# Top-k attention and two feed-forward layers: the second layer of token chunk 1 in float16 parts, and the weight splits reordered

## The chip, the cores and the metric

The kernel runs on one core of one Trainium2 chip. The metric is device time in microseconds, as a median over runs. A core has a matrix engine (TensorE, PE in the rows; its weight loads are shown apart as PEld), VectorE (DVE), ScalarE (ACT), GpSimd (POOL), and a queue (SP) from which all transfers are issued here. Each engine works through its own instructions in order and waits on the others by semaphores.

## The reference

Attention over 4 batches, 8 heads, 576 positions and head size 64 keeps the 32 largest scores of each row. Its output, 2304 tokens of width 512, goes through a gated layer of width 1536 and then a squared-ReLU layer of width 2048.

```
scores = scale * q @ k.T                       # (4, 8, 576, 576)
kth = the 32nd largest of each row
attn = softmax(scores where scores >= kth)
x = (attn @ v) as (2304, 512)
x = (sigmoid(x @ w_gate) * (x @ w_val)) @ w_out      # 512 -> 1536 -> 512
r = max(x @ w_in, 0);  out = (r * r) @ w_out2        # 512 -> 2048 -> 512
```

Everything is float32 at the interface.

## The kernel before

Tokens are worked in twelve chunks (`CHUNKS`): chunks 0 to 5 of 128 tokens, chunks 6 to 11 of 256. For each chunk the attention gives x transposed, 128 x 4 x N, and then two feed-forward layers follow: here called layer 1 (weights `wg`, `wv`, `wo`) and layer 2 (`wi`, `w2`, the latter for `w_out2`).

There are two forms of these layers. `moe32` (L982) works chunks 0 and 1 (`PLAIN`) with float32 products straight from the float32 weights. `moe` (L862) works the others: each float32 operand is there as two float16 parts, high and low, scaled by powers of two, and each product is three float16 products (`SPLIT`: high by high, high by low, low by high). In layer 2 of both forms eight pairs of blocks of 128 hidden units are passed (`l2_pair`, L931 in `moe` and L1048 in `moe32`), and their squared ReLU is multiplied with `w2` (`l2_acc`). `moe` keeps three pairs in hand before it sums (`DEPTH2`), `moe32` one. Lines 938 and 959 are the two products of layer 2 in `moe`; lines 1052 and 1069 are those in `moe32`, and line 1045 is the copy between layer 1 and layer 2 there. In `moe`, lines 911 and 912 write the two parts of layer 2's input x2. For chunks from 6 on x2 is scaled by a bound that `x_norm` (L800) gets from the squares of x (`x_squares`, L789); for chunks 2 to 5 a fixed power of two (`X2B`) is used.

The weights come first as float32 pairs of blocks (`conv`, names `wg_c`, `wi_c` and so on; 34 pairs: 6 of wg, 6 of wv, 6 of wo, 8 of wi, 8 of w2). `scale` finds a power of two for each matrix. `split` (L714) makes the float16 parts of one pair, names `wg_w`, `wi_w` and so on (w2's pairs appear as `w_c` and `w_w`): ACT writes the high part (L718), and then DVE the low part (L721) or, for every third split (`LOP`), POOL in two steps (L723, L724). A pair and its parts are buffers of the same size in one pool of 35 (`WSLOTS`); the parts need a free one, and the pair's buffer comes free when it has been split and read by everyone. The first two pairs of wo lie in another pool of three buffers, tag `m4`, where x of the chunks lies as well (`x_plain` for chunks 0 and 1, then `xt_2`, `xt_3` and so on).

The order of all work is found when the program is built: instructions are emitted with priorities, and a scheduler with a simulated time line places them in each engine's order. The loop at the end of the program (from L1338) interleaves three streams by hand-set times: steps of the weights (`weight_step`), units of the attention (`att`, one block of 128 rows and one head) and steps of `moe32` (`body`). The counter `n` counts the steps of a chunk's body: 6 pairs of layer 1, 8 pairs of layer 2, one end. The list `todo` says at which step of chunk 1 each split is emitted; the splits have a time far behind (`SUP`), so they fill in where engines are free. Before, wg and wv come from step 2, wo from step 3, wi from step 8 and w2 from step 9 on. What is left is emitted after chunk 1. Chunks 2 to 11 follow in the last loop, with the attention kept ahead of them.

In the attention each row block needs four MAX8 and three MATCH_REPLACE8 on DVE (L434, L435) for its 32 largest scores, transposes on TensorE that pass through a PSUM pool of two buffers (`ps_t`, tag `tr`), and the product with v, which passes through the same pool and is then copied into x by ACT (`values`, copy at L594).

Of the kernel before, what the change touches and what calls it, by code (L numbers as in the profile page):

```python
# [72 lines left out]
PB = 10  # L73
XF = 2
# [17 lines left out]
def tile_topk_attention__then__two_moe_layers(  # L92
# [694 lines left out]
    x2s = {}  # L787

    def x_squares(ci, xt, after=None):  # L789
# [3 lines left out]
        ins = nc.scalar.activation(sq, xt[:, 0], AF.Square)  # L793
# [6 lines left out]
    def x_norm(ci, sq, N, after=None):  # L800
# [61 lines left out]
    def moe(ci, nxt=None):  # L862

        m = ahead.pop(ci)
        tts, N, ix, l1_pair = chunks[ci], m.N, m.ix, m.l1_pair
        accs = []

        def l1_acc(fp, gh):
            if not accs:
                for h in range(2):  # L870
                    accs.append(ps_a.tile([P, 512], F32, tag="acc", name=f"acc1_{ci}_{h}"))

            last = fp == NF1 // 2 - 1
            for e, d in sorted(
                ((e, d) for e in range(2) for d in range(KM)),
                key=lambda t: (t[1], t[0]) if last else t,
            ):
                f = 2 * fp + e
                if True:
                    for x, (a, b_) in enumerate(SPLIT):  # L880
                        nc.tensor.matmul(  # L881
                            accs[d // 2][:, (d % 2) * N : (d % 2 + 1) * N],
                            wblk("wo", a, f, d * P, P),
                            gh[:, b_, e * N : (e + 1) * N],
                            start=(f == 0 and x == 0 and d % 2 == 0),
                            stop=(f == NF1 - 1 and x == 2),
                            skip_group_check=True,
                        )

        queue = m.queue  # L890
        depth = max(1, len(queue))
        for fp in range(len(queue), NF1 // 2):
            queue.append((fp, l1_pair(fp)))
            yield
            if len(queue) > depth:
                l1_acc(*queue.pop(0))
        while len(queue) > 1:
            l1_acc(*queue.pop(0))
        if nxt:
            nxt()  # L900
        l1_acc(*queue.pop(0))

        pool, kw = (wpool, {"tag": "w"}) if ci >= X2W else (mpool, {"tag": "m4", "bufs": M4})
        x2 = pool.tile([P, 2, KM, N], F16, name=f"x2_{ci}", **kw)
        KH = KM // 2
        srcs = [a[:, 0 : KH * N].rearrange("p (d n) -> p d n", d=KH) for a in accs]
        with tc.high_priority(offset=XUP):
            sy, iy = x2s.pop(ci, (float(2.0**-X2B), float(2.0**X2B)))
            for h in range(2):
                hs = slice(h * KH, (h + 1) * KH)  # L910
                nc.scalar.activation(x2[:, 0, hs], srcs[h], AF.Copy, scale=sy)
                nc.vector.scalar_tensor_tensor(
                    x2[:, 1, hs], srcs[h], sy, x2[:, 0, hs], op0=ALU.mult, op1=ALU.subtract
                )
        if nxt:
            for _ in range(NPRE - 1):
                nxt()
# [61 lines left out]
        yield  # L979


    def moe32(ci, xt):  # L982
# [60 lines left out]
        l1_acc(*prev)  # L1043
        x2 = xt
# [60 lines left out]
    def attention():  # L1105
# [62 lines left out]
        def tail(n, after=None):  # L1168
# [277 lines left out]
```

## Time and profile before

| | us |
|---|---|
| median of 3 runs | 1189.3 (1188.53 to 1190.75) |
| the profiled execution, time | 1192.72 |
| the profiled execution, span from first to last instruction | 1190.9 |
| busy in the span: TensorE | 1150.0 (97%) |
| DVE | 912.2 (77%) |
| ACT | 796.2 (67%) |
| POOL | 831.5 (70%) |
| mean granted clock of TensorE | 0.991 |

Busy times count each engine's instructions; matmuls are pipelined, so the length of one matmul is longer than the distance from its start to the next one's start. A float32 product shows as two records. The rows further down come from the page, from the tables by stretch, from the time lines of single engines and from the groups by line or tile. In a time line a row with x16 stands for sixteen instructions in a run; its second number is from the first start to the last end.

### The profile page before, as it was taken

The page shows a single profiled execution, that of the slowest core. Times are in us where ns is not written, and L with a number is a line of the kernel's source. Part 1 is how long each engine was busy: PE and PEld are TensorE (multiplying, and loading weights), DVE is VectorE, ACT ScalarE, POOL GpSimd, SP SyncE. Part 2 cuts the span into 40 slices and gives each one's busy share as a digit, 9 for nine tenths or more (in the row PEclk, how much of TensorE's full clock was granted, in tenths as well). Part 3 has the DMA queues.
Part 4 walks back from the last instruction along what each step waited for, and adds up shares of the span by engine and source line. Part 5 has one row for each costly group of instructions (what it writes and reads, how often), then busy time and mean ns, then how long its engine had stood idle before and what let it go on. Part 6 is the DMA issues. An engine that isn't in the chain of part 4 may idle for free.

```text
span 1190.9 us, 30480 instructions
## 1 busy us (share of the span) xinstructions
PE 1150.0 (97%) x11457; PEld 936.0 (79%) x11457; DVE 912.2 (77%) x1905; ACT 796.2 (67%) x1681; POOL 831.5 (70%) x1294
## 2 busy tenths in 40 slices
PE   7879999999999999999999999999999999999998
PEld 5668878978878878787887688868876886886785
DVE  5998789899998998999998899999799966110000
ACT  5999985778787787767677776777577665222122
POOL 1888874688877797969778887886698668224233
PEclk9888999999999999999999999999999999999999
DMA  7997854225435667765576576555255323000000
GB/s 228 364 362 251 311 159 128 80 71 154 122 104 132 134 155 159 173 140 137 120 161 132 132 189 123 138 126 125 61 119 116 78 57 61 19 1 1 19 1 18
DMA packets 241395, 153.64 MB, mean 129 GB/s; under 512 B 191329, under 2 KB 207713, under 8 KB 241249
## 3 DMA queue, kind: packets, MB, share of 16 engines
q1 hardware_dynamic: 241248, 151.70, 49.2%
q8 instruction: 90, 1.47, 0.5%
q14 instruction: 57, 0.46, 0.1%
HBM read 105.25 MB, written 18.09 MB: 104 GB/s over the span
## 4 chain that ended last, share of the span: by engine, by line
PE 52%; SPq 1%; POOL 1%; DMA 1%; issue 1%; ACT 1%; DVE 0%; POOLq 0%; ACTq 0%
PE ph L938 11%; PE acc L959 11%; PE acc L881 7%; PE pg L841 7%; PE pv L841 7%; PE sp L423 3%; PE xp L559 3%; PE qpt L383 1%; SPq L344 1%; DMA kst<-ks 1%; PE kpt L197 0%; DVE W L435 0%; SPq L214 0%; DVE mx L434 0%; PE xn L803 0%
## 5 line engine op out<-in xcount | busy, mean ns | idle before, releaser
L434 DVE MAX8 mx<-W 128x8 f32<-128x576 f32 x432 | 327.5, 758 | 10.4
L435 DVE MATCH_REPLACE8 W<-mx,W 128x576 f32<-128x576 f32 x288 | 213.7, 742 | 0.0
L938 PE MATMUL ph<-x,wi_w 128*128 128x256 f16 (+1 forms) x1920 | 190.7, 251 | 0.0
L959 PE MATMUL acc<-w_w,rh 128*128 128x512 f16 x768 | 181.1, 379 | 1.4 <-POOL rh L951 1.4
L938 PEld LDWEIGHTS <-wi_w 128*128 128x128 f16 x1920 | 154.9, 98 | 24.6 <-issue 0.7
L506 POOL TENSOR_TENSOR pp<-S,pp 128x512 f16<-128x512 f32 x192 | 137.1, 736 | 1.9
L423 PE MATMUL sp<-kst,qt 128*128 128x288 f32 x608 | 130.1, 327 | 4.5 <-ACT S L426 3.1
L460 ACT ACTIVATE S<-S,mx 128x576 f32<-128x576 f32 x144 | 111.8, 776 | 33.5 <-DVE mx L434 32.5
L959 PEld LDWEIGHTS <-rh 128*128 128x128 f16 x768 | 72.3, 98 | 74.9 <-POOL rh L951 2.2
L841 PEld LDWEIGHTS <-wg_w 128*128 128x128 f16 x1440 | 118.1, 98 | 15.8 <-issue 1.1
L881 PEld LDWEIGHTS <-wo_w 128*128 128x128 f16 x1440 | 118.0, 98 | 14.8 <-issue 1.8
L841 PEld LDWEIGHTS <-wv_w 128*128 128x128 f16 x1440 | 117.1, 98 | 15.0 <-issue 2.6
L853 DVE TENSOR_TENSOR th<-pv,th 128x512 f32<-128x512 f32 (+1 forms) x60 | 34.6, 576 | 118.5 <-PE pv L841 110.5
L434 DVE MAX8 mx<-S 128x8 f32<-128x576 f32 x144 | 107.1, 744 | 21.2 <-ACT S L426 21.0
L426 ACT COPY S<-sp 128x576 f32<-128x576 f32 x144 | 91.8, 638 | 45.2 <-PE sp L423 22.1
L504 POOL TENSOR_SCALAR S<-S,bs 128x576 f32<-128x576 f32 x96 | 71.9, 749 | 52.1 <-ACT pp L503 45.8
L435 DVE MATCH_REPLACE8 W<-mx,S 128x576 f32<-128x576 f32 x144 | 106.9, 742 | 0.0
L950 POOL TENSOR_TENSOR r<-r 128x512 f32<-128x512 f32 (+1 forms) x80 | 70.5, 881 | 49.1 <-ACT rh L949 47.4
L841 PE MATMUL pv<-xs,wv_w 128*128 128x256 f16 x864 | 104.7, 273 | 0.0
L503 ACT ACTIVATE pp<-S,bs 128x576 f16<-128x576 f32 x96 | 74.5, 776 | 44.4 <-DVE bs L499 22.1
L841 PE MATMUL pg<-xs,wg_w 128*128 128x256 f16 x864 | 104.0, 273 | 0.0
L881 PE MATMUL acc<-gh,wo_w 128*128 128x256 f16 (+1 forms) x1056 | 102.5, 248 | 0.0
(240 smaller groups left out, 2307.0 us busy)
## 6 DMA issues: line engine op xcount, KB each, us to landing
kst<-ks SPq DMA_DIRECT2D x112, 288.0 KB, 3.2
v<-vd SPq DMA_DIRECT2D x32, 320.0 KB, 3.4
wi_r<-in_moe_w_in_dram SPq DMA_DIRECT2D x16, 512.0 KB, 5.0
w_r<-in_moe_w_out_dram SPq DMA_DIRECT2D x16, 512.0 KB, 4.9
qn<-in_q_dram SPq DMA_DIRECT2D x124, 64.0 KB, 2.6
v<-in_v_dram SPq DMA_DIRECT2D x28, 256.0 KB, 2.8
wg_r<-in_moe_w_gate_dram SPq DMA_DIRECT2D x12, 512.0 KB, 5.9
wv_r<-in_moe_w_val_dram SPq DMA_DIRECT2D x12, 512.0 KB, 7.8
```

The source lines that it names most:

```text
L423: nc.tensor.matmul(sp[:, e, 0:HALF], l, r, start=(x == 0), stop=(x == len(ops) - 1))
L426: nc.scalar.copy(ss.rearrange("p (e s) -> p e s", e=2), sp[:, :, 0:HALF])
L434: return nc.vector.max(m8, st.cur).ins
L435: ins = nc.vector.match_replace(st.wk, m8, st.cur, NEG).ins
L460: nc.scalar.activation(wk, wk, AF.Prelu, bias=kth, scale=-1.0, alpha=1.0 / BIG)
L503: nc.scalar.activation(pp[:, 0:S], wk, AF.Copy, scale=rz)
L504: nc.gpsimd.tensor_scalar(wk, wk, rz, 1.0, op0=ALU.mult, op1=ALU.mult)
L506: nc.gpsimd.tensor_tensor(pp[:, o : o + e - f], wk[:, f:e], pp[:, f:e], op=ALU.subtract)
L841: nc.tensor.matmul(pp[:, e * N : (e + 1) * N], wblk(wd, a, c, f0, P), xs[:, b_, c, :], start=(e == 0 and n == 0), stop=(n == 3 * KM - 1), ...
L881: nc.tensor.matmul(accs[d // 2][:, (d % 2) * N : (d % 2 + 1) * N], wblk("wo", a, f, d * P, P), gh[:, b_, e * N : (e + 1) * N], start=(f == ...
L938: nc.tensor.matmul(ph[:, e * N : (e + 1) * N], wblk("wi", a, c, f0, P), x2[:, b_, c, :], start=(e == 0 and n == 0), stop=(n == 3 * KM - 1) ...
L959: nc.tensor.matmul(acc2[i][:, 0:DM], gh[:, b_, e * N + i * P : e * N + (i + 1) * P], wblk("w2", a, f, 0, DM), start=(f == 0 and x == 0), s ...
```

## The change

Chunk 1 (`SPLIT2`) keeps its float32 layer 1. Its layer 2 now runs the code of `moe`, which is moved into a function `layer2` for that. The result of layer 1 is scaled by `f`, a product of powers of two from the norm of chunk 1's x and the scales of wv and wo, and written as two float16 parts over x's own buffer (two ACT and two DVE operations on halves, where one ACT copy was). The norm comes from `x_squares` and `x_norm`, which are now called for chunk 1 as well when its x is complete.

Chunk 1 thus needs wi and w2 split before its layer 2. The list `todo` is emitted along both chunks, with `n2` = 15 steps for chunk 0: wi from step 10 of chunk 0 (`SWI`), w2 from step 1 of chunk 1 (`SW2`), wg and wv from step 2 of chunk 1 and wo from step 3 as before. Entries with the same step keep the order in which they are listed, so wo's first pair is the nineteenth entry; before it was the fifth.

```diff
+SPLIT2 = (1,)
+SWI = 10
+SW2 = 1
...
-        ins = nc.scalar.activation(sq, xt[:, 0], AF.Square)
+        ins = nc.scalar.activation(sq, xt if ci in SPLIT2 else xt[:, 0], AF.Square)
...
-        t = xsmall[ci]
+        if ci in SPLIT2:
+            t = mpool.tile([P, 8], I32, tag="xsc", bufs=3, name=f"xn_{ci}s")
+        else:
+            t = xsmall[ci]
         cm = t.bitcast(F32)[:, 3:4]
         nc.vector.reduce_max(cm, pq[:, 0:N], axis=AX.X)
+        if ci in SPLIT2:
+            xnorm[ci] = pow2_scale(cm, t)
+            return
...
+    def layer2(ci, x2, ix, iy):
...
         l1_acc(*prev)
+        if ci in SPLIT2:
+            s, ix = xnorm.pop(ci)
+            sv, so = (scales[n][0] for n in ("wv", "wo"))
+            f = wsmall.bitcast(F32)[:, 21:22]
+            nc.vector.scalar_tensor_tensor(
+                f, s, float(2.0 ** -(TB + X2B)), sv, op0=ALU.mult, op1=ALU.mult
+            )
+            nc.vector.tensor_tensor(f, f, so, op=ALU.mult)
+            x2 = xt.rearrange("p c n -> p (c n)").bitcast(F16).rearrange(
+                "p (a c n) -> p a c n", a=2, c=KM
+            )
+            src = accs[0][:, 0 : KM * N].rearrange("p (d n) -> p d n", d=KM)
+            KH = KM // 2
+            for h in range(2):
+                hs = slice(h * KH, (h + 1) * KH)
+                nc.scalar.activation(x2[:, 0, hs], src[:, hs], AF.Copy, scale=f)
+                nc.vector.scalar_tensor_tensor(
+                    x2[:, 1, hs], src[:, hs], f, x2[:, 0, hs], op0=ALU.mult, op1=ALU.subtract
+                )
+            yield from layer2(ci, x2, ix, float(2.0**X2B))
+            return
...
                     if pr.ci in PLAIN:
                         xsp[pr.ci] = pr.xt
+                        if pr.ci in SPLIT2:
+                            x_squares(pr.ci, pr.xt)
...
+    n2 = n1 + NF2 // 2 + 1
+    for i in range(len(pairs_of["wi"])):
+        todo.append((max(SWI, n1 + 2 * (i // 2) + 2), "wi", i))
+    for i in range(len(pairs_of["w2"])):
+        todo.append((n2 + SW2 + i // 2, "w2", i))
     for i in range(len(pairs_of["wg"])):
-        todo.append((2 * (i // 2) + 2, "wg", i))
-        todo.append((2 * (i // 2) + 2, "wv", i))
+        todo.append((n2 + 2 * (i // 2) + 2, "wg", i))
+        todo.append((n2 + 2 * (i // 2) + 2, "wv", i))
     for i in range(len(pairs_of["wo"])):
-        todo.append((i + 3, "wo", i))
-    for i in range(len(pairs_of["wi"])):
-        todo.append((n1 + 2 * (i // 2) + 2, "wi", i))
-    for i in range(len(pairs_of["w2"])):
-        todo.append((n1 + i + 3, "w2", i))
-    todo = [(max(t[0], TD), *t[1:]) for t in todo]
+        todo.append((n2 + i + 3, "wo", i))
     todo.sort(key=lambda x: x[0])
...
-                if ci == PLAIN[-1]:
-                    at(tm - SUP)
-                    while todo and todo[0][0] <= n:
-                        split(*todo.pop(0)[1:])
+                at(tm - SUP)
+                while todo and todo[0][0] <= n + n2 * (ci == PLAIN[-1]):
+                    split(*todo.pop(0)[1:])
```

## Rows read from the trace of the kernel before

**Rows 1.** Engines by stretch: busy us (x count), granted clock, DMA share, GB/s.

```profile
140.00:280.00 140.00, 139.36 (x1150) 116.20 (x1150) 120.14 (x228) 104.10 (x204) 98.43 (x134) 1.00 0.42 120
280.00:540.00 260.00, 248.70 (x3464) 215.60 (x3464) 242.17 (x534) 198.84 (x474) 207.40 (x372) 1.00 0.59 142
540.00:1010.00 470.00, 469.54 (x4608) 371.39 (x4605) 419.28 (x878) 331.87 (x692) 373.45 (x614) 1.00 0.53 117
1010.00:1191.00 181.00, 177.13 (x1414) 136.27 (x1413) 11.15 (x20) 41.50 (x66) 55.49 (x55) 1.00 0.04 11
```

**Rows 2.** Timelines (start us, length us, engine, line) around the input of chunk 2.

```profile
181.58 1.09 PE L586 MATMUL xp<-PT,v 128*64 128x128 f32 x16
...
200.37 3.08 DVE L721 SCALAR_TENSOR_TENSOR wo_w<-wo_c,wsmall,wo_w 128x1024 f16<-128x1024 f32 x1 [0.27 <-ACT wo_w L718]
...
204.42 0.27 ACT L594 COPY xt<-xp 128x128 f32<-128x128 f32 x1
...
240.22 1.18 POOL L783 TENSOR_TENSOR xt<-xt 128x512 f16<-128x512 f32 x1
...
275.70 0.50 PE L841 MATMUL pg<-xt,wg_w 128*128 128x128 f16 x6
```

**Rows 3.** Groups of PE by line, 237 to 280: count, busy us, mean ns.

```profile
L1052 PE MATMUL ph<-x_plain,wi_c 128*128 128x128 f32 x128 | 16.5, 276 | 0.1
L1069 PE MATMUL acc<-w_c,rr 128*128 128x512 f32 x32 | 15.3, 594 | 0.0
```

**Rows 4.** Timeline of PE, second layer of chunk 1, three runs in a row.

```profile
247.38 1.95 PE L1052 MATMUL ph<-x_plain,wi_c 128*128 128x128 f32 x16
249.17 1.88 PE L1069 MATMUL acc<-w_c,rr 128*128 128x512 f32 x4
250.89 0.38 PE L1052 MATMUL ph<-x_plain,wi_c 128*128 128x128 f32 x2
```

**Rows 5.** Timeline of PE, second layer of chunk 2, two runs and what follows.

```profile
322.63 2.41 PE L938 MATMUL ph<-x,wi_w 128*128 128x128 f16 x40
324.85 0.77 PE L423 MATMUL sp<-kst,qt 128*128 128x288 f32 x4
...
333.30 2.75 PE L959 MATMUL acc<-w_w,rh 128*128 128x512 f16 x12
335.89 0.61 PE L938 MATMUL ph<-x,wi_w 128*128 128x128 f16 x8
```

**Rows 6.** Groups of PE by line, 320 to 355 (chunk 2).

```profile
L938 PE MATMUL ph<-x,wi_w 128*128 128x128 f16 x192 | 13.0, 219 | 0.0
L959 PE MATMUL acc<-w_w,rh 128*128 128x512 f16 x48 | 11.9, 380 | 0.0
```

**Rows 7.** Tile acc: count, ns min/median/max, first and last start us.

```profile
L911 ACT ACTIVATE x<-acc x8: 363/392/418, 320.6 to 531.5; 128x256 f16<-128x256 f32 x8
L912 DVE SCALAR_TENSOR_TENSOR x<-acc,x x8: 405/412/425, 321.8 to 532.8; 128x256 f16<-128x256 f32 x8
```

**Rows 8.** The page's groups: idle us ahead of the sums of layer 2.

```profile
L959 PE MATMUL acc<-w_w,rh 128*128 128x512 f16 x768 | 181.1, 379 | 1.4 <-POOL rh L951 1.4
```

**Rows 9.** Line 718, the splits on ACT: count, ns, first and last start us.

```profile
L718 ACT ACTIVATE wi_w<-wi_c,wsmall x8: 1148/1149/1151, 258.2 to 310.6; 128x1024 f16<-128x1024 f32 x8
L718 ACT ACTIVATE w_w<-w_c,wsmall x8: 1133/1149/1157, 265.0 to 324.6; 128x1024 f16<-128x1024 f32 x8
L718 ACT ACTIVATE wg_w<-wg_c,wsmall x6: 1148/1150/1156, 167.5 to 235.9; 128x1024 f16<-128x1024 f32 x6
L718 ACT ACTIVATE wo_w<-wo_c,wsmall x6: 1134/1149/1150, 199.2 to 253.0; 128x1024 f16<-128x1024 f32 x6
```

**Rows 10.** Timeline of ACT, the third and the fourth split.

```profile
174.37 1.15 ACT L718 ACTIVATE wg_w<-wg_c,wsmall 128x1024 f16<-128x1024 f32 x1
...
197.40 1.15 ACT L718 ACTIVATE wv_w<-wv_c,wsmall 128x1024 f16<-128x1024 f32 x1 [1.10 <-PE pg L997]
```

**Rows 11.** Weight loads of the float16 second layer, ns min/median/max.

```profile
L938 PEld LDWEIGHTS <-wi_w x1920: 95/98/105, 321.4 to 1176.4; 128*128 128x128 f16 x192
```

More of the change, by code (lines that the diff above doesn't have):

```diff
@@ L787, in tile_topk_attention__then__two_moe_layers @@
     x2s = {}
+    xnorm = {}
     def x_squares(ci, xt, after=None):
@@ L860, in moe_head @@
         m.N, m.ix, m.l1_pair = N, ix, l1_pair
[L862 to L917, printed above, removed]
@@ L918, in moe @@
+    def layer2(ci, x2, ix, iy):
+        tts = chunks[ci]
+        N = len(tts) * P
         usc, i2 = layer2_scales()
@@ L979, in moe, with l1_acc @@
         yield
+    def moe(ci, nxt=None):
+        m = ahead.pop(ci)
+        N, ix, l1_pair = m.N, m.ix, m.l1_pair
+        accs = []
+        def l1_acc(fp, gh):
+            if not accs:
+                for h in range(2):
+                    accs.append(ps_a.tile([P, 512], F32, tag="acc", name=f"acc1_{ci}_{h}"))
+            last = fp == NF1 // 2 - 1
+            for e, d in sorted(
+                ((e, d) for e in range(2) for d in range(KM)),
+                key=lambda t: (t[1], t[0]) if last else t,
+            ):
+                f = 2 * fp + e
+                if True:
+                    for x, (a, b_) in enumerate(SPLIT):
+                        nc.tensor.matmul(
+                            accs[d // 2][:, (d % 2) * N : (d % 2 + 1) * N],
+                            wblk("wo", a, f, d * P, P),
+                            gh[:, b_, e * N : (e + 1) * N],
+                            start=(f == 0 and x == 0 and d % 2 == 0),
+                            stop=(f == NF1 - 1 and x == 2),
+                            skip_group_check=True,
+                        )
+        queue = m.queue
+        depth = max(1, len(queue))
+        for fp in range(len(queue), NF1 // 2):
+            queue.append((fp, l1_pair(fp)))
+            yield
+            if len(queue) > depth:
+                l1_acc(*queue.pop(0))
+        while len(queue) > 1:
+            l1_acc(*queue.pop(0))
+        if nxt:
+            nxt()
+        l1_acc(*queue.pop(0))
+        pool, kw = (wpool, {"tag": "w"}) if ci >= X2W else (mpool, {"tag": "m4", "bufs": M4})
+        x2 = pool.tile([P, 2, KM, N], F16, name=f"x2_{ci}", **kw)
+        KH = KM // 2
+        srcs = [a[:, 0 : KH * N].rearrange("p (d n) -> p d n", d=KH) for a in accs]
+        with tc.high_priority(offset=XUP):
+            sy, iy = x2s.pop(ci, (float(2.0**-X2B), float(2.0**X2B)))
+            for h in range(2):
+                hs = slice(h * KH, (h + 1) * KH)
+                nc.scalar.activation(x2[:, 0, hs], srcs[h], AF.Copy, scale=sy)
+                nc.vector.scalar_tensor_tensor(
+                    x2[:, 1, hs], srcs[h], sy, x2[:, 0, hs], op0=ALU.mult, op1=ALU.subtract
+                )
+        if nxt:
+            for _ in range(NPRE - 1):
+                nxt()
+        yield from layer2(ci, x2, ix, iy)
     def moe32(ci, xt):
@@ L1043, in moe32 @@
         l1_acc(*prev)
+        if ci in SPLIT2:
[8 more added lines that the diff above has]
+                "p (a c n) -> p a c n", a=2, c=KM
+            )
+            src = accs[0][:, 0 : KM * N].rearrange("p (d n) -> p d n", d=KM)
+            KH = KM // 2
+            for h in range(2):
+                hs = slice(h * KH, (h + 1) * KH)
+                nc.scalar.activation(x2[:, 0, hs], src[:, hs], AF.Copy, scale=f)
+                nc.vector.scalar_tensor_tensor(
+                    x2[:, 1, hs], src[:, hs], f, x2[:, 0, hs], op0=ALU.mult, op1=ALU.subtract
+                )
+            yield from layer2(ci, x2, ix, float(2.0**X2B))
+            return
         x2 = xt
```

## The prediction, made before the change was run

> **What bounds the kernel now.** The median is 1189.3 us; the profiled execution took 1192.7 us, of which the span is 1190.9. All durations below come from that execution, so sums are made against 1192.7 and then carried to the median, 3.4 us lower. I read the busy time of the engines by stretch first. The reader is to see that TensorE (PE) is idle for 0.6 us of the 140 us between 140 and 280, for 11.3 us of the 260 between 280 and 540, for 0.5 us of the 470 after that, and that its granted clock is 1.00 in all four stretches, the higher level of 2.4 GHz [rows 1]. VectorE (DVE) has 20 us to spare in the first of these stretches and 51 us in the third, and after 1010 it does 11 us of work in 181. So from about 140 us on TensorE has a backlog, and the time after that point is the sum of its work plus some 16 us of gaps. Whatever is taken from TensorE there comes off the end, unless it turns into a gap.
>
> That the backlog is real is seen at chunk 2: the low part of its input, the last thing that its first layer needs from the attention, is written at 240.22 + 1.18 = 241.4 us, and its first product is issued at 275.70 [rows 2]. TensorE is 34 us behind its supply.
>
> **The change part by part.**
>
> *Second layer of chunk 1 in float16 parts.* This layer lies between 237 and 280 us, inside the stretch where TensorE never rests. Before, it has 64 float32 products of 128 columns and 16 of 512. Each shows as two records: 128 and 32 records in this stretch [rows 3]. Their pace, from start to start in an unbroken run: 16 records in 249.17 - 247.38 = 1.79 us, 0.112 each, and 4 in 250.89 - 249.17 = 1.72 us, 0.430 each [rows 4]. So 128 x 0.112 + 32 x 0.430 = 14.3 + 13.8 = 28.1 us. After, it has 3 products for each: 192 of 128 columns and 48 of 512. Chunk 2, which has the same 128 tokens and already runs this code, shows the pace: 40 in 324.85 - 322.63 = 2.22 us, 0.0555 each, and 12 in 335.89 - 333.30 = 2.59 us, 0.216 each [rows 5]. So 192 x 0.0555 + 48 x 0.216 = 10.7 + 10.4 = 21.0 us. Saved: 7.1 us. The groups by line say the same in another way, with the overlaps at the ends of runs counted in: 16.5 + 15.3 = 31.8 us [rows 3] against 13.0 + 11.9 = 24.9 us [rows 6], 6.9 us. I take 7.1, the pace: how often the schedule switches between kinds of products after the change is not known.
>
> *The norm of x for chunk 1.* Four products of 128 columns with ones, 4 x 0.0555 = 0.2 us. The squaring on ScalarE (ACT), one reduction and the tiny scale operations run between the arrival of x for chunk 1 and its use after the whole first layer; they are needed only at the start of the second layer, so I cost them at nothing. Without that cover they would cost one hand-over more, as priced next.
>
> *From layer 1 to layer 2.* One ACT copy becomes two ACT copies and two DVE operations on halves; chunk 2's show 0.39 us for each of the first and 0.41 for each of the second [rows 7]. TensorE needs the high half at once and the low half 8 products later. Bounds: 0, if score products and transposes fill the place as they do at chunk 2, and 2 x 0.39 + 2 x 0.41 = 1.6 us in a row, with as much again for the search operations that DVE has queued ahead: 3.2 us. I take 0.5, near the lower end, since at chunk 2 there is attention work in that very place.
>
> *Per pair of blocks.* ACT squares once more and POOL subtracts once more, eight times; TensorE has three pairs in hand before it needs a result (DEPTH2 = 3, against one before), and the ten chunks that run this code, 80 pairs, show 1.4 us of TensorE idle ahead of these sums in all [rows 8], so nothing is added.
>
> *The splits, moved.* All 34 stay, with the same work: ACT 1.15 us each [rows 9], then DVE, or POOL for every third. The order changes: wi goes first, from step 10 of chunk 0, then w2 is mixed with wg, wv and wo. No DMA moves. Before, three splits are issued by 174.37 and the next at 197.40 [rows 10]: the three free weight buffers are taken, and the next comes free only when chunk 1 has read wg and wv. After, wi can be split right behind chunk 0's last use of it and gives its buffer back, so this hole of 23 us can hold splits (some five or six: between 197.4 and 253.0 the other 15 of the 18 splits of wg, wv and wo were issued, one in 3.7 us [rows 9, 10]). The cost: ACT, DVE and POOL are fuller between 165 and 250 and emptier between 265 and 326, where w2 and most of wi were split [rows 9]. TensorE is not touched directly. But one queue is: the split of wo's first pair, now fifth, becomes nineteenth. Chunk 2's input lives in the buffer that this pair gives back: the product that fills it is begun at 181.58, the split runs from 200.37 to 203.45, and the copy into xt starts only at 204.42 [rows 2]. Behind this copy stand a PSUM buffer of two, hence all transposes of the attention. When the attention stalls there, DVE and ACT are free for splits, so the eleven that would still be due at 197 (nineteen less three and five) would go at little over ACT's 1.15 us each; I expect the copy some 10 us later. TensorE has 34 us of backlog to cover that, less 7. Without that cover each us late would cost one.
>
> Sum: -7.1 + 0.2 + 0.5 + 0 = -6.4: 1186.3 for a profiled execution, 1182.9 for the median, called 1183.0.
>
> **The rivals.**
>
> *Late input, slower.* If the wo split is not sped up by the stall, 11 splits at 3.7 us from 197 put it at 238, and with it the copy some 35 us late. Chunk 2 is reached 7 us earlier, and attention products that are held back (what the second layer leaves of TensorE between 237 and 280: 43 - 31.8 = 11 us, a quarter [rows 3]) let it come earlier still, so TensorE runs dry when the delay D passes (34 - 7)/1.26 = 21 us, and each further us costs 1.26. The point from which the kernel is slower by over 0.2% is a gap of 6.4 + 2.4 = 8.8 us, D = 28. Half way from there to the worst, D = 31.5, the gap is 13.2 us: 1183.0 + 13.2 = 1196.2. For it: the order of the list. Against: before, the splits hurried in exactly such a stall. Chance 0.11.
>
> *DVE takes over, no change.* Between 280 and 540 DVE is busy 242 of 260 us [rows 1]. If a TensorE that is 7 us early only waits there for scores and transposed weights, the gaps of 11.3 us grow by 5 or so: about 1188.0. Against: the splits leave this stretch at the same time. Chance 0.12.
>
> *Weight loads set the pace, no change.* Three float16 products need 192 weight loads where the float32 layer had 128. A float16 load lasts 98 ns [rows 11]. If products came at the pace of their loads, 192 x 0.098 = 18.8 us plus 10.4 makes 29.2 against 28.1: 1.1 us lost, 1190.6. Against it stand 40 products in 2.22 us. This is the change not doing what it says. Chance 0.04. The Trainium skill, "TensorE: Matmul & The Clock Gate", section "Back-to-back issue gap", gives about 81 ns a product for a sustained stream of weight loads and products at 128 columns, and about 131 ns at 512. By its first figure the 192 products would take 15.6 us and the gain would be 2 us; by both together 21.8 us and a gain of about 6. The trace disagrees with both figures: 55.5 and 216 ns [rows 5].
>
> *More than the products.* Chunk 2's second layer begins at 321 [rows 7] while w2 is still being split, until about 326 [rows 9]. With wi and w2 done early, ACT, DVE and POOL serve chunk 2 and the search better, and a third of the 11.3 us of gaps could go: 1179.3. Chance 0.16.
>
> **How the numbers follow.** The forecast itself, 1183.0 within 2.5 us either way (the bounds of the hand-over and of the norm), has 0.57. Faster, by over 0.2% (2.4 us, about what a measurement of this kernel can tell from no change): 0.57 + 0.16 = 0.73. Within 0.2%: 0.12 + 0.04 = 0.16. Slower: 0.11. The range of 1178.5 to 1190.5 takes in the larger gain and both cases of no change but not the late input; it leaves out about 0.15.
>
> **What would show it.** TensorE's busy time falls by about 7 us; the lines of the second layer show 128 float32 records instead of 256 and 32 instead of 64; runs of 128 columns keep 55.5 ns. TensorE's gaps between 140 and 280 stay under 2 us; chunk 2's first product comes near 269. The first copy into xt comes before 224. I am wrong if gaps in front of chunk 2's products by a split or by x appear, if the gaps between 280 and 540 grow by as much as the products saved, or if the span falls by much more than TensorE's busy time.

## The result and the profile after

The changed kernel takes 1204.69 us (median of 4 runs, 1203.02 to 1206.72) against 1190.03 for the kernel before, run beside it: a ratio of 1.0117, interval 1.0096 to 1.0137. It is slower by 14.7 us, where 1183.0 was forecast. Its profiled execution took 1206.72 us with a span of 1204.9, against 1190.9. The ratios here and below are worked out from the single executions of both kernels and need not equal the quotient of the two medians. In two kernels below one execution was far longer than all others (4846.01 and 1899.15 us), and these two are left out of the medians.

The engines by stretch of the changed kernel, answering to [rows 1] (columns: stretch, its length, busy us and count of PE, PEld, DVE, ACT and POOL, granted clock, DMA share, GB/s):

```profile
140.00:280.00 140.00, 126.20 (x1139) 106.95 (x1138) 122.50 (x213) 106.59 (x201) 116.54 (x128) 0.96 0.38 107
280.00:540.00 260.00, 248.90 (x3416) 214.41 (x3414) 236.04 (x539) 191.85 (x469) 191.00 (x374) 0.99 0.59 145
540.00:1010.00 470.00, 468.06 (x4642) 374.77 (x4641) 421.90 (x886) 331.00 (x694) 367.32 (x605) 1.00 0.53 118
```

The loss stands in the first row. TensorE was idle there for 0.6 us and is now idle for 13.8; GpSimd went from 98.4 us of work to 116.5; the granted clock fell from 1.00 to 0.96. The later rows hardly differ from before: gaps of 11.1 us against 11.3 between 280 and 540, 1.9 against 0.5 after that. In finer slices of the same view:

```profile
180.00:200.00 20.00, 17.80 (x128) 14.56 (x129) 17.69 (x35) 13.18 (x23) 14.28 (x13) 0.83 0.38 96
200.00:220.00 20.00, 16.14 (x126) 15.71 (x125) 18.73 (x25) 14.30 (x21) 19.66 (x17) 0.91 0.31 86
220.00:240.00 20.00, 18.39 (x173) 17.00 (x172) 18.12 (x30) 14.48 (x25) 17.06 (x17) 1.00 0.30 76
240.00:260.00 20.00, 16.00 (x175) 14.06 (x174) 19.83 (x39) 17.20 (x34) 14.54 (x19) 1.00 0.33 83
```

GpSimd is full in 200 to 220 (19.66 of 20). What TensorE waited for between 160 and 280 (total us, times, longest), the four largest:

```profile
PE acc L1038 <- DVE g L1028: 4.7, 2, 3.9
PE sp L426 <- POOL qt L402: 3.9, 2, 2.8
PE sp L426 <- ACT qt L398: 2.6, 2, 1.5
PE ph L895 <- ACT x_plain L1074: 1.4, 1, 1.4
```

In the first two the longest wait leads back to a split on GpSimd. Here is that of the second, in the time line of the changed kernel (start us, length us, engine, line; the bracket is the idle time before, and who ended it). L724 is the low part of a split on VectorE, L727 on GpSimd, L402 a small step of the attention (`qt`, the low part of the queries) that TensorE's scores need:

```profile
176.63 1.27 DVE L724 SCALAR_TENSOR_TENSOR wi_w<-wi_c,wsmall,wi_w 128x1024 f16<-128x1024 f32 x1
176.66 3.24 POOL L727 TENSOR_TENSOR wi_w<-wi_c,wi_w 128x1024 f16<-128x1024 f32 x1
178.50 2.49 DVE L724 SCALAR_TENSOR_TENSOR wi_w<-wi_c,wsmall,wi_w 128x1024 f16<-128x1024 f32 x1
179.86 1.59 POOL L1099 TENSOR_TENSOR rr<-r 128x256 f32<-128x256 f32 x1
181.42 0.72 POOL L402 TENSOR_TENSOR qt<-qn,qt 128x256 fp32r<-128x256 f32 x1
182.20 1.09 PE L426 MATMUL sp<-kst,qt 128*128 128x288 f32 x3 [2.81 <-POOL qt L402]
```

The split holds GpSimd from 176.66 to 179.90, a step of chunk 0's layer 2 follows, and only then comes the 0.72 us for which TensorE stands still for 2.81 us. The longest of the first is of the same kind, with VectorE between. L1026 and L1028 make the gate and the gated product `g` that the sums of layer 1 (L1038) need:

```profile
204.55 3.09 POOL L727 TENSOR_TENSOR w_w<-w_c,w_w 128x1024 f16<-128x1024 f32 x1
207.61 0.40 POOL L1026 TENSOR_SCALAR th<-th 128x256 f32<-128x256 f32 x1
208.05 0.42 DVE L1028 TENSOR_TENSOR g<-pg,th 128x256 f32<-128x256 f32 x1 [1.07 <-POOL th L1026]
208.53 3.68 PE L1038 MATMUL acc<-g,wo_c 128*128 128x128 f32 x16 [3.86 <-DVE g L1028]
```

The layer itself did what it was meant to do. Its two groups (count, busy us, mean ns, idle us before), answering to [rows 3] and [rows 6]:

```profile
L895 PE MATMUL ph<-x_plain,wi_w 128*128 128x128 f16 x192 | 13.7, 219 | 1.4 <-ACT x_plain L1074 1.4
L916 PE MATMUL acc<-w_w,rh 128*128 128x512 f16 x48 | 12.1, 380 | 0.0
```

And the input of chunk 2, answering to [rows 2]:

```profile
218.55 0.27 ACT L597 COPY xt<-xp 128x128 f32<-128x128 f32 x1 [1.42 <-DVE wo_w L724]
...
263.21 1.16 POOL L786 TENSOR_TENSOR xt<-xt 128x512 f16<-128x512 f32 x1
...
282.27 0.50 PE L851 MATMUL pg<-xt,wg_w 128*128 128x128 f16 x6
```

The first copy comes 14 us later than before, but the finished input still waits 18 us for TensorE. It is not what TensorE ran dry on; between 160 and 280 TensorE waited 0.5 us in all for a copy into xt.

### The profile page after: what moved, and what is told of

Its sections match the earlier page's. It is cut to its first block, busy times and chain, and to the rows that moved or that the text cites. A ratio compares the mean times of both kernels' runs of the same rounds, so it can differ in the third digit from the quotient of the medians.

```text
span 1204.9 us, 30687 instructions
## 1 busy us (share of the span) xinstructions
PE 1149.3 (95%) x11541; PEld 937.5 (78%) x11541; DVE 917.5 (76%) x1915; ACT 799.0 (66%) x1691; POOL 840.5 (70%) x1302
## 5 line engine op out<-in xcount | busy, mean ns | idle before, releaser
L916 PE MATMUL acc<-w_w,rh 128*128 128x512 f16 x816 | 194.5, 379 | 0.1
L895 PEld LDWEIGHTS <-wi_w 128*128 128x128 f16 x2112 | 166.6, 98 | 28.1 <-issue 2.0
L916 PEld LDWEIGHTS <-rh 128*128 128x128 f16 x816 | 76.5, 98 | 76.0 <-POOL rh L908 0.8
L907 POOL TENSOR_TENSOR r<-r 128x512 f32<-128x512 f32 (+1 forms) x88 | 75.4, 857 | 48.5 <-ACT rh L906 46.7
L426 PEld LDWEIGHTS sp<-kst,qt 128*128 128x128 f32 x608 | 89.7, 191 | 19.1 <-POOL qt L402 4.8
```

The source lines that it names most:

```text
L426: nc.tensor.matmul(sp[:, e, 0:HALF], l, r, start=(x == 0), stop=(x == len(ops) - 1))
L895: nc.tensor.matmul(ph[:, e * N : (e + 1) * N], wblk("wi", a, c, f0, P), x2[:, b_, c, :], start=(e == 0 and n == 0), stop=(n == 3 * KM - 1) ...
L907: nc.gpsimd.tensor_tensor(r, r, r, op=ALU.mult)
L916: nc.tensor.matmul(acc2[i][:, 0:DM], gh[:, b_, e * N + i * P : e * N + (i + 1) * P], wblk("w2", a, f, 0, DM), start=(f == 0 and x == 0), s ...
```

## The experiments

Two questions were put: which part of the change costs, and where the 7 us of products went. All times below are medians beside runs of the kernel before on the same chip (1189.7 to 1191.0), each followed by the ratio and its 95% interval.

### Each part alone

The float16 layer alone, with the splits in the order of before (`todo` as before; layer 2 of chunk 1 reads parts that exist by then):

```diff
+    def otherblk(name, a, kt, f0, n):
+        return wblk("wg", a, kt % KM, f0 % 512, n)
...
+        blk = otherblk if ci in SPLIT2 else wblk
```

> Chunk 1's second layer runs the float16 code of the changed kernel, but the splits keep the order and the steps of the kernel before; since wi and w2 are not yet split then, this layer reads parts of wg in their place (its output rows are left wrong). Theory (the splits stand in front of small operations in the queues of POOL, DVE and ACT while they are packed into 165 to 265 us): the layer by itself saves what was worked out, about 6 us, so 1182 to 1187, and TensorE is idle for under 3 us between 160 and 280. Rival 1 (the layer itself, its norm, its hand-over and its extra ACT and POOL work, brings the gaps): 1195 or more, with gaps between 160 and 280. Rival 2 (chunk 2's input comes late because of wo's first pair): here the pair is split as before, so 1182 to 1187 too.

Measured: 1189.62, ratio 0.9997 (0.9978 to 1.0015). The layer by itself brings nothing that can be measured; the 3 to 8 us expected did not come, and neither did the loss of the first rival.

The splits alone, with chunk 1's float32 layer 2 on constants (the same is done for `w2`):

```diff
-SPLIT2 = (1,)
+SPLIT2 = ()
...
-                        fblk("wi", c, (2 * fp + e) * P, P),
+                        ident if ci == PLAIN[-1] else fblk("wi", c, (2 * fp + e) * P, P),
```

> The splits stand where the changed kernel has them, but chunk 1's second layer stays in float32 products of the same count and shape; since wi and w2 are already split and their float32 pairs gone, it reads constants in their place (its output rows are left wrong). Theory: gaps and slow clock between 160 and 250 as in the changed kernel and no products saved, so about 1204.7 + 6.5 = 1211, range 1206 to 1214. Rival 1 (the layer brings the gaps): about 1189 to 1192. Rival 2 (late input): 1208 to 1214 as well, it differs in the run with wo's first pair in front.

Measured: 1202.85, ratio 1.0095 (1.0075 to 1.0114), below the range of 1206 to 1214 but far above the rival's. Nearly the whole loss belongs to the moved splits. TensorE's longest wait in this trace is another one than in the changed kernel: 6.4 us for a step of VectorE (`kn`, the low part of the keys), which stands in VectorE's own queue behind a split that lasts 2.42 us beside one on GpSimd:

```profile
201.89 3.17 POOL L727 TENSOR_TENSOR w_w<-w_c,w_w 128x1024 f16<-128x1024 f32 x1
203.71 2.42 DVE L724 SCALAR_TENSOR_TENSOR wv_w<-wv_c,wsmall,wv_w 128x1024 f16<-128x1024 f32 x1
206.73 0.67 DVE L211 TENSOR_TENSOR kn<-kpt,kp 128x512 fp32r<-128x512 f32 x1
207.45 0.36 PE L200 MATMUL kpt<-ident,ke 64*128 64x64 f32 x1 [6.44 <-DVE kn L211]
```

So it is not one small step, nor GpSimd's queue alone, that the packed splits hold up.

### What in the splits costs

None of the splits on GpSimd (`LOA = 34` in place of 0, changed kernel):

> The changed kernel, but no split uses POOL: all low parts are written by DVE (LOA = 34). Theory, in the form that POOL splits of 3.3 us and more stand ahead of POOL's small steps (the query parts, the gate) and that DVE and POOL stretch each other's splits when they overlap: the gaps that end on POOL go, TensorE's idle time between 160 and 280 falls from 13.8 to about 6 us, 1193 to 1198. Rival (DVE is simply overfull there, whoever splits): DVE gets 10 more low parts of 1.27 us, the gaps stay or grow: 1204 to 1215.

Measured: 1191.59, ratio 1.0009 (0.9990 to 1.0027): 13 us of the 14.7 come back, more than expected. But this edit also plans the order anew, and it brings the first copy into xt back to 206.5 us.

wo's first pair split early again, as in the kernel before:

```diff
-        todo.append((n2 + i + 3, "wo", i))
+        todo.append((n2 + i + 3 if i else 9, "wo", i))
```

> The changed kernel, with wo's first pair split first instead of nineteenth, so that chunk 2's first x is not held back for it. Rival 2 (the late copy into xt and the transposes behind it hold the attention up, and this costs TensorE): 1190 to 1198, the copy into xt near 204. Theory (the queues): the gaps ahead of 218 stay; 1202 to 1207.

Measured: 1194.36, ratio 1.0029 (1.0010 to 1.0047), with the first copy into xt back at 203.9 us. The edit gave back 10 us, which is the range of the late copy and not that of the queues. Yet it shifts which splits are every third one, and the order of everything behind; so this run alone proves nothing on wo, and it does not refute the late copy either.

GpSimd's splits in four pieces each, so that small steps might pass between them (changed kernel):

```diff
-            nc.gpsimd.tensor_scalar(c, c, s, 1.0, op0=ALU.mult, op1=ALU.mult)
-            nc.gpsimd.tensor_tensor(t[:, 1], c, t[:, 0], op=ALU.subtract)
+            for e in range(2):
+                for q in range(2):
+                    cs = c[:, e, q * 256 : (q + 1) * 256]
+                    hi, lo = (t[:, a, e, q * 256 : (q + 1) * 256] for a in range(2))
+                    nc.gpsimd.tensor_scalar(cs, cs, s, 1.0, op0=ALU.mult, op1=ALU.mult)
+                    nc.gpsimd.tensor_tensor(lo, cs, hi, op=ALU.subtract)
```

> The changed kernel, but each split on POOL is cut into four pieces of 128x256, so that POOL's small steps need to wait for 0.3 to 0.6 us of a split instead of 2.1 to 3.2. The work on POOL and what DVE and POOL take from each other when both split stays the same. Theory that the stall is a matter of queue order (a small step of POOL stands behind a whole split): most of what the run without POOL splits gained comes here too, 1192 to 1197. Rival (DVE and POOL slow each other down, and the sum of the work is too much): 1201 to 1206.

Measured: 1207.26, ratio 1.0144 (1.0111 to 1.0177), above both ranges. Shorter single steps did not help here, though this order too is planned anew. The wait for `qt` grows from 3.9 us to 7.5:

```profile
PE sp L426 <- POOL qt L402: 7.5, 3, 4.3
```

and GpSimd is full for longer (the last busy figure of each stretch):

```profile
180.00:200.00 20.00, 17.30 (x125) 13.61 (x124) 16.35 (x31) 13.10 (x23) 19.22 (x28) 0.93 0.38 103
200.00:220.00 20.00, 18.38 (x138) 18.11 (x139) 16.72 (x26) 13.73 (x22) 19.39 (x31) 0.83 0.28 74
```

No splits on GpSimd, and the hand-over from layer 1 to layer 2 at high priority (the loop over its halves inside `with tc.high_priority(offset=int(AUP * 50))`):

> The changed kernel without POOL splits, and with the four steps that write chunk 1's x2 emitted at high priority, so that no split and no search step stands ahead of them. In the run without POOL splits TensorE waited 1.65 us for the second high half and 1.30 us for a low half, with a slower clock behind it. Theory (each gap in this stretch costs its length): 3 to 4 us less than that run, 1187 to 1189. Rival (gaps here are made up or come back later): 1191 to 1193.

Measured: 1191.85, ratio 1.0021 (1.0002 to 1.0040). The hand-over still cost 1.7 and 1.3 us of waits; nothing was gained, and as the waits did not shrink, what a quicker hand-over is worth stays open.

The control, the same `LOA = 34` in the kernel before:

> The kernel before with all 34 splits' low parts on VectorE (none on GpSimd), the control for the same edit on the changed kernel, which took that one from 1204.7 to 1191.6. If GpSimd's share hurts only where splits are packed into the first chunk (my reading), before has nothing to win: 1188 to 1193. If a split on GpSimd costs anywhere, before becomes faster too: 1180 to 1186, and the 13 us are then not all the change's. If VectorE is short in 190 to 330, it becomes slower: 1194 or more.

Measured: 1188.13, ratio 0.9985 (0.9966 to 1.0004). Splits on GpSimd cost little or nothing where they stood before; as far as two kernels with orders of their own can tell, most of the 13 us of the third run are the change's own.

Every edit so far changes the planned order of all engines, which is a cause of its own (below). So the next kernels were changed after the order was set: every engine keeps its instructions in the same sequence, and only the sizes of some are cut. First the changed kernel, GpSimd's splits shortened (the scaling to 64 of 1024 columns, the subtraction to 512 words that leave zeros):

```diff
+    for blk in nc.m.functions[0].blocks:
+        for n, x in enumerate(blk.instructions):
...
+            if x.opcode == "TensorTensor" and _re.match(r"(wi|w2|wg|wv|wo)_w\d", m):
...
+                blk.instructions[n] = _dc.replace(x, ins=[h, h], outs=[o])
```

> The changed kernel with every engine's instructions in the changed kernel's order; only the sizes of GpSimd's split instructions are changed after the order is set: the scaling to 64 of 1024 columns, and the subtraction to one over 512 words that leaves zeros (so these weights have no low part). That takes some 2.2 us off each of 11 splits on GpSimd. If GpSimd's time in splits is what costs (small steps of attention behind them, and VectorE slowed beside them): 1190 to 1196, the gaps of 160 to 280 fall from 13.8 to under 6 us, VectorE's splits back near 1.3 us. If the order that is planned around 16 more splits in the first two chunks is what costs, whatever they take: 1200 to 1206. Between the two, both have a share, and the number gives it.

Measured: 1190.04, ratio 0.9991 (0.9970 to 1.0012): the whole loss is gone, with not one instruction in another place. So the price was GpSimd's time in the splits, as the new order places them, and what follows from it; beside the 1189.62 of the same layer in the old order, the new order by itself shows no cost. Two things were not run: the same shortening in the kernel before, so how much of the 15 us would come off there too is known only from the control above; and a kernel with the first copy into xt held late but the splits short (here it comes at 207.6), so against the late copy there are only the waits read above. No wait for `qt` on GpSimd is left between 160 and 280; the longest that remains is again for `g`:

```profile
PE acc L1038 <- DVE g L1028: 2.5, 1, 2.5
```

This run's stretches 180 to 240 and 240 to 300:

```profile
180.00:240.00 60.00, 56.10 (x490) 51.22 (x489) 56.75 (x103) 49.14 (x85) 35.91 (x50) 0.97 0.36 101
240.00:300.00 60.00, 58.44 (x724) 49.33 (x724) 58.36 (x130) 43.87 (x105) 40.61 (x83) 1.00 0.36 107
```

The same two stretches of the changed kernel:

```profile
180.00:240.00 60.00, 52.33 (x422) 47.27 (x423) 54.54 (x88) 41.96 (x68) 50.99 (x45) 0.91 0.33 86
240.00:300.00 60.00, 54.48 (x598) 44.85 (x596) 58.76 (x114) 45.23 (x104) 41.50 (x72) 1.00 0.36 103
```

With 15 us less of GpSimd's work in 180 to 240, TensorE's gaps shrink from 7.7 to 3.9 us there and from 5.5 to 1.6 in the next 60; not to nothing, as expected, since 1.4 us of hand-over and others stay. The granted clock is 0.97 where it was 0.91. TensorE executes the same instructions in both, and is busy 1149.3 us in the changed kernel and 1142.8 in this one: about 6.5 us of the loss are products at the lower clock (its mean over the span is 0.986 against 0.991, which makes some 6 us by itself).

VectorE gains as well. Its splits (L724) in 180 to 240 (length of the stretch, busy us and count, clock, DMA share, GB/s), first in the changed kernel:

```profile
180.00:240.00 60.00, 27.43 (x15) 0.91 0.33 86
```

then with GpSimd's splits shortened:

```profile
180.00:240.00 60.00, 21.43 (x16) 0.97 0.36 101
```

and with none on GpSimd (the third run):

```profile
180.00:240.00 60.00, 31.73 (x25) 0.97 0.36 93
```

That is 1.83, 1.34 and 1.27 us for each. Where GpSimd splits too, in full length, those on VectorE last 0.56 us longer on average. Shortening GpSimd's splits takes away this lengthening and the small steps' wait in GpSimd's queue together; how the 15 us divide between the two was not separated.

### Where the 7 us of products went

Half of chunk 1's w2 sums left out of the kernel before, 6.9 us of TensorE's work:

```diff
-            for e in range(2):
+            for e in range(1 if ci == PLAIN[-1] else 2):
```

> The kernel before, with half of the sums of chunk 1's float32 second layer left out (8 products of 512 columns, 16 records of 0.430 us: 6.9 us of TensorE's work; its output rows are left wrong). Nothing else is moved or added. Theory of the prediction (TensorE has a backlog there, so what is taken off comes off the end): 1183, 6.9 us less than before. Rival, after the run of the layer alone gave 0.4 us instead of 6.4 (TensorE's queue is interleaved there with attention steps that come at the pace of ACT, DVE and POOL, so time saved turns into gaps): 1186 to 1190.

Measured: 1196.63, ratio 1.0069 (1.0043 to 1.0096): less work, and slower by 6.9 us, which neither theory nor rival had.

A third of chunk 8's layer 2 sums left out instead:

```diff
+                    terms = SPLIT[:2] if ci == 8 else SPLIT
```

> The kernel before, with a third of the sums of layer 2 of chunk 8 left out (32 float16 products of 512 columns at 0.216 us: 6.9 us; its output rows are left a little wrong). It is the control for the run with less work in chunk 1: the same amount is taken in a stretch where TensorE shows 30.0 busy in 30. Both theories: 1183, all of it comes off. If less than 5 us comes off here, a busy TensorE is not a bound anywhere before the last chunks.

Measured: 1184.75, ratio 0.9964 (0.9943 to 0.9984): 4.3 us of 6.9 come off there, by the ratio (5.0 by the medians; the interval allows 1.9 to 6.8). That is at the line of 5 us that was drawn, so it does not decide whether all of a saving comes off there; some of it does.

Why the one and not the other? Both plan the order anew from the place of the edit on: against the kernel before, the engines' sequences first differ at 247 to 259 us in the first of them, and only at 875 to 887 us in the second, when most of the attention is done. So the same place was lightened with the order kept, 15 of the 16 w2 products of chunk 1 at half their columns:

```diff
+            if x.opcode == "Matmult" and x.outs[0].memref.startswith("acc2_1_"):
...
+                w = _dc.replace(w, ap=[w.ap[0], [1, 256]])
+                o = _dc.replace(o, ap=[o.ap[0], [1, 256]])
```

> The kernel before with every engine's instructions in the order of before; only the sizes of 15 of the 16 float32 products of chunk 1's w2 sums are changed after the order is set, from 512 to 256 output columns (so half the columns of chunk 1's result lack those terms). A float32 product of 512 columns took four passes of 216 ns, so the edit takes 15 x 0.43 = 6.5 us of work off TensorE between 190 and 285, at the place where the change itself saves 7.1. My forecast's theory (TensorE is the bound there and its work is what counts): 1183 to 1185.5. The rival that the other engines give the pace in this stretch, so that freed time turns into waits for small steps of attention: 1187.5 to 1191, with 4 us or more of new gaps in 140 to 300. If the 7 us that less work cost in the run where half of these sums were left out came from the order planned anew, this kernel isn't slower than before; if it is at 1195 or above, planning anew was not the cause.

Measured: 1191.19, ratio 0.9994 (0.9977 to 1.0010). Not slower, so the loss of the run with half of these sums left out came from the order planned anew; and not faster either. The stretches of the kernel before (columns as above):

```profile
180.00:240.00 60.00, 59.36 (x533) 53.96 (x531) 54.06 (x100) 39.95 (x74) 33.19 (x46) 1.00 0.36 100
240.00:300.00 60.00, 58.60 (x550) 47.73 (x549) 58.83 (x111) 46.44 (x95) 51.09 (x74) 1.00 0.39 114
300.00:360.00 60.00, 59.16 (x818) 49.90 (x818) 58.27 (x126) 48.23 (x115) 47.80 (x82) 1.00 0.43 119
```

and of the lightened one:

```profile
240.00:300.00 60.00, 54.29 (x553) 48.22 (x552) 58.56 (x110) 46.30 (x94) 50.79 (x75) 1.00 0.38 114
```

TensorE's gaps in 240 to 300 grow from 1.4 to 5.7 us: 4.3 of the 6.5 us are given back at once. VectorE is the likely reason: in the kernel before it is busy 58.8 of 60 us there and 58.3 in the next 60. Its time line does not get ahead. Three of its splits in the kernel before:

```profile
272.06 1.27 DVE L721 SCALAR_TENSOR_TENSOR wi_w<-wi_c,wsmall,wi_w 128x1024 f16<-128x1024 f32 x1
275.43 1.27 DVE L721 SCALAR_TENSOR_TENSOR wi_w<-wi_c,wsmall,wi_w 128x1024 f16<-128x1024 f32 x1
284.80 1.27 DVE L721 SCALAR_TENSOR_TENSOR w_w<-w_c,wsmall,w_w 128x1024 f16<-128x1024 f32 x1
```

and the same in the lightened kernel, with TensorE's first product of chunk 2:

```profile
272.32 1.27 DVE L721 SCALAR_TENSOR_TENSOR wi_w<-wi_c,wsmall,wi_w 128x1024 f16<-128x1024 f32 x1
274.09 0.50 PE L841 MATMUL pg<-xt,wg_w 128*128 128x128 f16 x6
275.69 1.27 DVE L721 SCALAR_TENSOR_TENSOR wi_w<-wi_c,wsmall,wi_w 128x1024 f16<-128x1024 f32 x1
285.06 1.27 DVE L721 SCALAR_TENSOR_TENSOR w_w<-w_c,wsmall,w_w 128x1024 f16<-128x1024 f32 x1
```

All three are 0.26 us later, as much as VectorE's other steps there, while chunk 2's first product is 1.6 us earlier than the 275.70 of [rows 2]. TensorE comes early to the attention's next scores and transposes, and these are not ready. The waits themselves end on a transfer of keys (1.6 us), on GpSimd (`qt` 1.5 us, the weights to be transposed 0.7 us) and on ScalarE's copies into xt (0.8 us), none on VectorE; that the search on VectorE sets the pace behind them is inferred from its unmoved time line.

If that is so, the saving must show once VectorE also has less to do. VectorE's splits cut to half their elements, the order still kept, with and without the narrow products:

```diff
+                    c = _dc.replace(i[0], ap=[i[0].ap[0], [1, 512]])
...
+                    blk.instructions[n] = _dc.replace(x, ins=[c, one, c], outs=[o])
```

> The kernel before in its own order, with only VectorE's 23 split subtractions cut to 512 words that leave zeros (these weights have no low part), and TensorE's work whole. If TensorE and VectorE are both full in this stretch, cutting VectorE alone takes off only part of the gaps of 11.3 us that stood between 280 and 540: 1184.5 to 1188.5. If VectorE alone is the bound there: 1179 to 1184. If neither: 1189 to 1191.

Measured (VectorE alone): 1186.10, ratio 0.9961 (0.9945 to 0.9977), in the range for both engines being full.

> The kernel before in its own order, with the 15 w2 products of chunk 1 at half their columns (6.5 us less for TensorE, as in the run that gained nothing) and, besides, VectorE's 23 split subtractions over 512 words that leave zeros instead of 1024 elements (so these weights have no low part): some 0.63 us off each, 14 us in all, about 10 of them between 220 and 330. Theory: in 220 to 540 VectorE's own queue of search steps and splits sets when the attention's products can go, beside TensorE, so that time taken off TensorE alone becomes gaps. Then with both cut the 6.5 us come off: 1181 to 1185.5. Rival, that another thing (ScalarE, GpSimd, transfers) gives the pace there: 1187.5 to 1191.

Measured (both): 1183.74, ratio 0.9941 (0.9917 to 0.9966), inside the range of the theory. In 240 to 300 the first of these two shows

```profile
240.00:300.00 60.00, 59.24 (x609) 48.24 (x606) 53.44 (x111) 49.42 (x100) 45.25 (x78) 1.00 0.37 108
```

and the second

```profile
240.00:300.00 60.00, 57.51 (x662) 52.22 (x659) 57.01 (x118) 49.76 (x103) 49.08 (x82) 1.00 0.39 115
```

TensorE's cut now leaves 1.7 us of new gaps in this stretch instead of 4.3, and takes 2.4 us off the time instead of nothing. The two intervals overlap, so the 2.4 us is likely rather than certain. What the traces show is plainer: with VectorE at 97 to 98%, TensorE's saving turns into gaps; with some slack on VectorE, less of it does. Shorter splits on VectorE also leave GpSimd freer (45.3 us of work in this stretch against 51.1), so the slack may not be VectorE's alone.

The same cut of VectorE's splits on top of GpSimd's in the changed kernel:

> The changed kernel in its own order with both GpSimd's split work cut (as in the run at 1190.0) and VectorE's split subtractions cut to 512 words (no weight has a low part). If the 7.1 us of the float16 layer were hidden by VectorE's queue: 1181 to 1185.5, and TensorE's gaps between 160 and 280 fall from that run's 6 us to under 3. If something else hides them: 1188 to 1191.

Measured: 1186.65, ratio 0.9977 (0.9960 to 0.9994), just outside the range of the theory; its interval overlaps that of the run with GpSimd's splits alone shortened. Its gaps in 180 to 240 are 3.2 us,

```profile
180.00:240.00 60.00, 56.76 (x542) 52.34 (x541) 51.10 (x110) 53.82 (x93) 30.77 (x56) 1.00 0.35 95
```

where ScalarE, which writes the high part of every split, has 53.8 us of work in 60; it had 40.0 in the kernel before. That it takes VectorE's place as the next limit is an inference from this row and was not tested.

## Why the prediction was wrong

*The step that failed: "ACT, DVE and POOL are fuller between 165 and 250 ... TensorE is not touched directly", at a cost of 0.* Measured by cutting GpSimd's splits in the unchanged order, its cost is 15 us (1.0117 against 0.9991 of the kernel before), as far as this cut would give nothing in the kernel before. The whole sum of GpSimd's work hardly changed (840.5 us against 831.5); but the splits entered queues in which the next `qt` or `th` of the critical work (with the splits alone, `kn` on VectorE) stood behind them, and where both engines split at once each split lasted longer. Which of the two costs more stays open. Looking at totals per stretch, as the prediction did, hides that: at 116.5 of 140 us GpSimd doesn't look full, and for 20 us it is.

*The backlog.* The prediction took the 34 us by which chunk 2's input stood ready [rows 2] for slack that covers everything. It is slack of one chain only. TensorE's queue holds layer products and the attention's products in one fixed order, and a score product that lacks its `qt` stops the layer products behind it, however long their inputs have been ready.

*"Whatever is taken from TensorE there comes off the end, unless it turns into a gap."* It turned into a gap. The prediction read 20 us of VectorE to spare in 140 to 280 [rows 1]. Nearly all of that lies before 240: in 240 to 300 VectorE is busy 58.8 of 60 us. One stretch cut differently would have shown two full engines.

*The layer: 7.1 us saved.* The size was right. The float16 products' groups show 25.8 us against 31.8 [rows 3], and with GpSimd's splits shortened, where the clock falls less, TensorE is busy 1142.8 us, 7.2 less than before. The step from busy time to time failed, by the point above: alone, the layer gave 0.4 us, within the noise, not 6.4.

*The hand-over: 0.5 us, between 0 and 3.2.* TensorE waited 1.4 us for it; inside the bounds, above the value taken.

*The wo split and chunk 2's input: about 10 us late, hidden.* The copy was 14 us late, and hidden: from 264.4 us, when the input is complete, to the first product at 282.3 there are still 18 us. With GpSimd's splits shortened and wo still nineteenth, the copy came at 207.6, so most of the delay was GpSimd's time and not the place in the list. That the lateness cost TensorE nothing is read from the waits; no run shows it by itself.

*The rivals.* "Late input" was the slower rival at 1196.2 and 0.11: the right sign by another mechanism, in another place, and short of the result. "DVE takes over", 1188.0 at 0.12, describes what became of 6.5 us of products in the kept order (1191.19), though in 240 to 300 and not between 280 and 540. For the layer alone (1189.62), whose order is planned anew, it is only half the answer: there VectorE is busy 54.7 of 60 us in 240 to 300 while TensorE has 4.9 us of gaps, and how much of them is the plan's wasn't separated. "Weight loads" fell: the layer's products last 219 and 380 ns, as at chunk 2. "More than the products" fell too: the gaps between 280 and 540 are 11.1 us against 11.3. The hidden saving was priced, by itself; the overfilled queues were not priced at all, and the case of both together had no place in the range.

*What was to show it.* TensorE's gaps between 140 and 280 are 13.8 us instead of under 2; its busy time falls by 0.7 us instead of 7, because the lower clock takes 6.5 back; the records are 192 and 48 float16 products instead of float32. Chunk 2's first product comes at 282.27, not 269. The first copy into xt, at 218.55, is before 224 as said.

No version that computes the whole result beats both kernels measurably; the nearest is the kernel before without splits on GpSimd, at 1188.13, whose interval takes in no change.

## What to carry to other kernels

Before taking work off the busiest engine, cut its stretch until the second one shows: where another in-order engine is as full, here at 97 to 98%, most of the saving can become gaps (4.3 of 6.5 us here), and it may have to be bought on both. When work moves to another time, add it, engine by engine, to what each queue already does in the new place, and look up which short steps of the critical work will stand behind it; the same total can cost 15 us. To tell an effect of length from one of planning, keep the planned order and change only the sizes.

## What the hardware showed that was not expected

VectorE's and GpSimd's splits take turns rather than share. In the time line at 176.63, VectorE's split starts 0.03 us ahead of GpSimd's: it lasts its usual 1.27 us, and GpSimd's lasts 3.24, which is 2.14 (its usual length) and 1.10. The next one on VectorE starts at 178.50 while GpSimd's still runs, until 179.90, and ends at 180.99: 2.49 us, 1.09 of them after GpSimd is done. The Trainium skill, "SBUF — State Buffer", section "Who interferes with whom", says that a VectorE instruction with two inputs in SBUF contends with a GpSimd instruction that reads SBUF, and that contention is over a port pair which the two share under an exclusive lock. The trace agrees: both orders occur in these three rows, and each time the later one lasts longer by about what was left of the other. The prediction did not weigh this; it speaks against packing splits on both engines into one stretch. The kernel before showed it already: VectorE's split of 3.08 us at 200.37 in [rows 2] has one of GpSimd beside it.

```profile
200.23 2.14 POOL L724 TENSOR_TENSOR wg_w<-wg_c,wg_w 128x1024 f16<-128x1024 f32 x1
```

TensorE's granted clock fell to 0.83 in 180 to 200 and 0.91 in 200 to 220 of the changed kernel, in a stretch with 6 us of gaps in 40, and was 1.00 again from 220. In slices of 2 us (busy us and count of TensorE, clock, DMA share, GB/s) it is 0.50, the lower of the two levels (1.2 GHz), right behind the two long waits of 2.81 and 3.86 us, which end at 182.20 and 208.53:

```profile
184.00:186.00 2.00, 2.00 (x18) 0.50 0.88 261
188.00:190.00 2.00, 2.00 (x8) 0.95 0.66 156
210.00:212.00 2.00, 2.00 (x11) 0.50 0.03 8
```

The gaps of 240 to 260, 4.0 us in all and none over 1.4, left it at 1.00. So the products ran at half speed from 182 to 188 and for some 3 us from 208.6 on, which is an estimate of 4.5 us lost, most of the 6.5 us by which TensorE's busy time differs from that of the same instructions with GpSimd's splits shortened.

Leaving out 6.9 us of work made the kernel 6.9 us slower when the order was planned anew, with TensorE waiting 8.0 us between 420 and 540 for transfers of the attention's weights (2.3 us in the kernel before):

```profile
PE xp L559 <- DMA PT<-pp: 8.0, 3, 2.8
```

So an edit's time includes a change of plan that can be as large as the edit itself.
